# Loading two expert weights by column halves, and writing 1280 output rows by halves

## The chip, the cores and the metric

The kernel runs on one core of a Trainium2 chip. The metric is the device time of one execution in microseconds, given as the median of several runs. The core's engines work from queues of their own and wait for one another through semaphores: TensorE (PE, matrix products into PSUM), VectorE (DVE), ScalarE (ACT), GpSimd (Pool) and SyncE (SP). 16 DMA engines move data between HBM and on-chip memory. In this kernel Pool issues every load and SP issues every store.

## The reference

A block-selecting attention over 4 batches of 8 heads (768 positions, head size 64) is followed by a soft mixture of 8 experts with 4 slots each. `x` is the attention's output, 3072 rows of 512.

```python
logits = x @ phi                      # 3072 x 32
d = softmax(logits, axis=0)           # over all rows
slot_input = (d.T @ x).reshape(8, 4, 512)
for e in range(8):
    h = np.maximum(slot_input[e] @ w1[e], 0.0)    # 4 x 1024
    slot_out[e] = h @ w2[e]                       # 4 x 512
c = softmax(logits, axis=1)
out = c @ slot_out.reshape(32, 512)   # 3072 x 512, float32
```

Because `d` is normalised over all rows, no expert can start before the last head of the last batch is done, and no output row can be made before all of `h @ w2` is summed, except by column halves: a column of the output needs only the same column of every `w2`.

## The kernel before

The attention loop runs over 16 pairs of heads (`i` from 0 to 15); its parts for several pairs are interleaved in an order written out by hand, and each engine does its work in that order. The weights are loaded beside it. Of the 16 matrices (1 MB each in bf16, cast from 2 MB of float32 in HBM), indices 0 to 7 are `w1` and 8 to 15 are `w2` in the order `LATE`, so that index 15 is expert 4. Line numbers are those of the profile. `load_w` (L144) loads a whole matrix in one DMA. `wplan` says how many matrices are issued in which `i`; index 14 is issued in `i` = 14. Index 15 alone is loaded by column halves in `i` = 15 (`load_w_half`, L150): `w_last[1]` (columns 256 to 511) first, then `w_last[0]`, each in two DMAs of 256 KB. All loads are on Pool's queue, between masks and other small work of Pool, and land in order of issue.

After the loop comes the tail. The last batch's logits and their softmax are made, the slots' inputs go into `siT_pad`, and `experts_in` (L852) forms the hidden layer in two halves `f` of 512 columns. `relu` (L859, ACT) and `hidden_T` (L864 on PE, copies L868 on DVE) put it transposed into `hT_pad`. Pool clears `siT_pad` (L774), `hT_pad` (L778) and `zrow` (L821) ahead of that and adds two small copies to `zrow` (L838, L839), from which `slot_sums` (L872, L873) makes `zinv`, the slots' normalisation.

The second product has three parts. `experts_out` (L891) does experts 0 to 3 over all 512 columns, in groups of 16 matmuls for each `f`, into `so_ps`, one PSUM bank. `shared_out` (L911) does experts 5 to 7 and `last_expert_out` (L921) expert 4, both for one column half `y` at a time: half 1 adds to `so_ps[:, 256:]`, half 0 goes to a tile of its own, `so_last`. So half 1 is complete first (L955, ACT, scales it into `so_sb[1]`); half 0 needs ACT's `so_part` (L956), the shared part, the last weight's half 0, and one DVE operation (L974) that adds both.

The output has 12 blocks of 256 rows. Blocks 0 to 2 (`BYHALF = 3`) are made by column halves: `out_half` multiplies by one half of the slots' output (L967), DVE (L944) and ACT (L941) scale 128 rows each into `o_tiles[m]`, and SP stores 256 KB (L969). Half 1 of blocks 0 and 1 comes before half 0 is complete. Blocks 3 to 11 are made over all columns (L986) and stored in 512 KB (L992), the last one in two pieces (L990). The pool `op` has five buffers `o_sb`; a block can only be written into a buffer whose store has landed. After block 4, `last_rows` makes the weights of the last batch's rows: transposes (L534), a DVE copy (L542), column sums (L759) and their reciprocal (L879).

PSUM has 8 banks: two double tiles `sc`, two single tiles `tp`, one double tile `at`.

Of the kernel before, what the change touches and what calls it, by code (L numbers as in the profile page):

```python
# [9 lines left out]
F32 = mybir.dt.float32  # L10
BF16 = mybir.dt.bfloat16
ALU = mybir.AluOpType
# [5 lines left out]
CH = 32  # L18
NCHUNK = 24
NQT = 6  # L20
P = 128
# [38 lines left out]
def kernel(  # L60
# [82 lines left out]
            dst = w_sb[i].rearrange("p (a f) -> p a f", a=NFG // 4)  # L143
        nc.gpsimd.dma_start(out=dst, in_=src)  # L144

    def load_w_half(t, y):

        src = moe_w2[LATE[E - 1]].rearrange("(a p x) d -> a p x d", p=P, x=4)
        for a in range(NFG // 4):
            nc.gpsimd.dma_start(  # L150
                out=t[:, 4 * a:4 * a + 4, :], in_=src[a, :, :, y * Dm // 2:(y + 1) * Dm // 2])

    def load(i, nm, n=1):

# [396 lines left out]
            step(i // NPB)  # L551


    wplan = {2: 1, 3: 1, 4: 1, 5: 1, 6: 1, 8: 1, 9: 1, 10: 1, 11: 1, 12: 1, 13: 2, 14: 1, 15: 1}
    nw = 2

    def weights(i):
        nonlocal nw
        for _ in range(wplan.get(i, 0)):
            load_w(nw)  # L560
            nw += 1
# [56 lines left out]
    for i in range(1, NPAIR):  # L618
        slots = have(i - 3) and (i - 3) % NPB == NPB - 1
        if i >= EARLY:  # L620
            wt = ctx.enter_context(tc.tile_pool(name=f"wt{i}", bufs=1))
            if i < LAST:
                w_sb.append(wt.tile([P, NFG * Dm], BF16, name=f"w_sb{i}"))
                weights(i)
            else:
                w_last = [wt.tile([P, NFG, Dm // 2], BF16, name=f"w_last{y}") for y in range(2)]
                for y in (1, 0):
                    load_w_half(w_last[y], y)
        scores(i, 0)
        expo(i, 0)  # L630
        moe(moe_max, i - 3)
        scores(i, 1)
        expo(i, 1)
        if have(i + 1):
            ubound(i + 1)
        if i < LAST - 1:
            moe(moe_bound, i - 3)
        if have(i - 2):
            normalise(i - 2)
        if i == LAST - 1:  # L640
            moe(moe_bound, i - 3)
        if i == LAST:
            moe_ct_copy(B - 2)
        if have(i + 1):
            select(i + 1)
        moe(moe_comb, i - 3)
        if have(i + 2):
            transposes(i + 2, "k")
            evac_T(i + 2, "k")
        if not slots:  # L650
            if have(i + 2):
                load_v(i + 2)
            if i < EARLY:
                weights(i)
        if i != LAST - 1:
            pv(i - 1, [0, 1, 2])
        for g in (2, 3):
            scores(i, g)
            expo(i, g, not slots)
            if g == 2 and i == LAST - 1:  # L660
                pv(i - 1, [0, 1, 2])
            if g == 2 and i == LAST:
                x_transposes(i - 2)
        moe(moe_exp, i - 3)
        if slots:
            mask(i, 2)
            mask(i, 3)
        if have(i - 2) and i < LAST:
            x_transposes(i - 2)
        pv(i - 1, [3])  # L670
        if have(i + 2):
            transposes(i + 2, "q")
            evac_T(i + 2, "q")
            kmin(i + 2)
        if i < LAST - 1:
            moe(moe_exp2, i - 3)
        if have(i - 2):
            evac_x(i - 2)
        if have(i + 2):
            kmax(i + 2)  # L680
        if i < LAST - 1:
            moe(moe_scale, i - 3)
        if slots:
            if have(i + 2):
                load_v(i + 2)
            if i < EARLY:
                weights(i)
        scores(i, 4)
        expo(i, 4)
        if have(i + 5) and i % 2:  # L690
            load(i + 5, "k", 2)
            load(i + 5, "q", 2)
        if i == LAST - 1:
            moe(moe_exp2, i - 3)
            moe(moe_scale, i - 3)
        if i == LAST:
            pv(i - 1, [4, 5])
        moe(moe_comb2, i - 3)
        scores(i, 5)
        expo(i, 5)  # L700
        if have(i + 1):
            ns_transposes(i + 1)
            evac_ns(i + 1)
        if i < LAST:
            pv(i - 1, [4])
        moe(moe_dispatch, i - 3)
        if i < LAST:
            pv(i - 1, [5])
        if have(i + 2):
            qsplit(i + 2)  # L710
        if i < LAST - 1:
            moe(moe_ct, i - 4)
        elif i == LAST - 1:
            moe(moe_ct, i - 3)
        moe(moe_logits, i - 2)
        moe(moe_copy, i - 2)
        if i == LAST - 2:
            l_ctx.close()
        if i == LAST - 1:
            u_ctx.close()  # L720
# [50 lines left out]
    evac_x(LAST, 3, NQT)  # L771
    moe_logits(BL, range(NDG - 1), lg12)
    moe_logits(BL, range(NDG - 1, NDG), lg12)
    nc.gpsimd.memset(siT_pad, 0.0)  # L774
    i_ctx.close()
    tail = ctx.enter_context(tc.tile_pool(name="tail", bufs=1))
    hT_pad = tail.tile([P, NFG, E, CH], BF16, name="hT_pad")
    nc.gpsimd.memset(hT_pad, 0.0)  # L778
    m_old = m_run[(BL + 1) % 2]
    pm = small.tile([P, NS], F32, name="pm", tag="pm")  # L780
    nc.vector.tensor_reduce(pm, lg1.rearrange("p t s -> p s t"), axis=AX.X, op=ALU.max)
# [35 lines left out]
    keep(2)  # L817

    si = st.pop("si")
    zrow = tail.tile([1, 4, CH], F32, name="zrow")  # L820
    nc.gpsimd.memset(zrow, 1.0)  # L821
    for g in range(2):
        sl = slice(g * 16, (g + 1) * 16)
        nc.vector.tensor_tensor(
# [54 lines left out]
        nc.vector.reciprocal(inv_b, ps)  # L879

    HD = Dm // 2
    so_ps = p_at.tile([P, 2, 512], F32, name="so_ps", tag="at")[:, 0, :]
    so_last = p_sc.tile([P, HD], F32, name="so_last", tag="sc")
    so_part = tail.tile([P, HD], F32, name="so_part")

    hT = hT_pad.rearrange("p f e c -> p f (e c)")

    def experts_out(f):
        for fg in range(f * 4, (f + 1) * 4):
            for e in range(4):  # L890
                nc.tensor.matmul(  # L891
                    so_ps[e * CH:(e + 1) * CH, :], lhsT=hT_pad[:, fg, e, :],
                    rhs=w_sb[E + e][:, fg * Dm:(fg + 1) * Dm], start=(fg == 0), stop=(fg == NFG - 1),
                )

    outs = (so_last, so_ps[:, HD:])

    SHARED = [
        [(5, 0), (5, 1), (5, 2)],
# [5 lines left out]
    def shared_out(y, f):  # L905
        for n in range(3):
            for j in range(4):
                e, fg = SHARED[j][n]
                fg += f * 4
                c0 = e * CH - (SPE if j == e - 5 else 0)  # L910
                nc.tensor.matmul(  # L911
                    outs[y][j * CH:(j + 1) * CH, :], lhsT=hT[:, fg, c0:c0 + CH],
                    rhs=w_sb[E + LATE.index(e)][:, fg * Dm + y * HD:fg * Dm + (y + 1) * HD],
                    start=(y == 0 and f == 0 and n == 0), stop=False, skip_group_check=(y == 1),
                )

    def last_expert_out(y):
        c0 = 4 * CH - 2 * SPE
        for fg in range(NFG):
            j = fg % 4  # L920
            nc.tensor.matmul(  # L921
                outs[y][j * CH:(j + 1) * CH, :], lhsT=hT[:, fg, c0:c0 + CH],
                rhs=w_last[y][:, fg, :],
                start=False, stop=(fg >= NFG - 4), skip_group_check=(y == 1),
            )

    experts_in(0, 0)
# [17 lines left out]

    w_ctx.close()
    op = ctx.enter_context(tc.tile_pool(name="op", bufs=5))
    experts_out(0)
    hidden_T(1)
    shared_out(1, 0)  # L950
    slot_sums()
    experts_out(1)
    shared_out(1, 1)
    last_expert_out(1)
    nc.scalar.activation(so_sb[1], so_ps[:, HD:], func=ACT.Copy, scale=zinv)  # L955
    nc.scalar.activation(so_part, so_ps[:, :HD], func=ACT.Copy, scale=zinv)  # L956
    shared_out(0, 0)
    shared_out(0, 1)

    BYHALF = 3  # L960
    o_tiles = [op.tile([P, 2, Dm], F32, name="o_sb", tag="o_sb") for _ in range(BYHALF)]

    def out_half(m, y, tags):
# [4 lines left out]
            scaled(o_tiles[m][:, x, cols], ps, 2 * m + x)  # L968
        nc.sync.dma_start(out=rows(m)[:, :, cols], in_=o_tiles[m][:, :, cols])  # L969

    out_half(0, 1, ("tp", "tp"))
    out_half(1, 1, ("sc", "at"))
    last_expert_out(0)
    nc.vector.scalar_tensor_tensor(so_sb[0], so_last, zinv, so_part, op0=ALU.mult, op1=ALU.add)  # L974
    out_half(2, 1, ("tp", "tp"))
    out_half(0, 0, ("sc", "at"))
    out_half(1, 0, ("tp", "tp"))
    out_half(2, 0, ("sc", "at"))

    n = 0  # L980
    for m in range(BYHALF, NM):
        o_sb = op.tile([P, 2, Dm], F32, name="o_sb", tag="o_sb")
        for x, scaled in enumerate((scaled_act, scaled_dve)):
            tag = ("sc", "tp", "tp", "sc", "at")[n % 5]
            o_ps = homes[tag].tile([P, Dm], F32, name="o_ps", tag=tag)
            nc.tensor.matmul(o_ps, lhsT=cT[:, m, x], rhs=so_all, start=True, stop=True)  # L986
            scaled(o_sb[:, x, :], o_ps, 2 * m + x)
            n += 1
            if m == NM - 1:
                nc.sync.dma_start(out=rows(m)[:, x], in_=o_sb[:, x, :])  # L990
        if m < NM - 1:
            nc.sync.dma_start(out=rows(m), in_=o_sb)  # L992
        if m == 4:
            last_rows()


# [28 lines left out]
```

## Time and profile before

| | us |
|---|---|
| median of 3 runs | 159.59 (158.88 to 159.78) |
| profiled execution | 158.52 |
| its span | 156.8 |
| PE busy | 136.5 |
| ACT busy | 122.8 |
| DVE busy | 121.9 |
| Pool busy | 98.7 |

The span is the part of the execution in which the profile shows work; the profiled time has 1.7 us around it. The profile gives each engine's busy time, a strip of 40 slices of 3.92 us each, the chain of work that ended last, and groups of instructions by line. A row of the timeline reads: start, duration, engine, line, operation, output and input, count, and in brackets the idle time before it and what ended it. "SPq" and "POOL ... DMA_DIRECT2D" rows are the issuing of a transfer, not the transfer; a DMA row's last number is the time from issue to landing. A row of a table by stretches reads: stretch, its length, busy time and count of PE, PEld (weight loads), DVE, ACT and Pool, then TensorE's clock, the DMA engines' busy share and the GB/s that they moved.

### The profile page before, as it was taken

What the parts mean: (1) busy time and instruction counts of PE and PEld (TensorE: products, weight loads), DVE (VectorE), ACT (ScalarE), POOL (GpSimd) and SP (SyncE); (2) the same over time, 40 slices, a digit from 0 to 9 for tenths busy, and PEclk for the clock granted to TensorE, in tenths of its full rate; (3) what the DMA queues carried; (4) which work ended last, traced back from release to release, by engine and by line L of the source; (5) the groups of instructions that cost most, each with busy time, mean ns of one, the idle gap of its engine ahead of it and who ended that gap; (6) DMA issues with size and microseconds to landing.
All of it is one profiled execution on the core that took longest, in us unless ns stands there. A gap on an engine that the chain in (4) does not pass through costs nothing.

```text
span 156.8 us, 5988 instructions
## 1 busy us (share of the span) xinstructions
PE 136.5 (87%) x2464; PEld 93.2 (59%) x2464; DVE 121.9 (78%) x437; ACT 122.8 (78%) x171; POOL 98.7 (63%) x192
## 2 busy tenths in 40 slices
PE   7796789999999999999999899999979999977500
PEld 4463466767766776766777677766657854633100
DVE  5478887999999998999899899999753761178720
ACT  3479899999999889999989999998789532276520
POOL 6999647958877876697597975869696810000000
PEclk9999999999999999999999999999999999999975
DMA  2999999999999999999999999999999999949995
GB/s 37 160 172 195 194 193 221 172 201 203 196 214 199 201 202 207 204 197 210 186 198 205 205 203 201 208 200 198 211 197 216 212 215 198 151 158 399 419 420 223
DMA packets 43131, 32.92 MB, mean 210 GB/s; under 512 B 26208, under 2 KB 37984, under 8 KB 43104
## 3 DMA queue, kind: packets, MB, share of 16 engines
q0 software_dynamic: 40032, 26.25, 113.9%
q1 hardware_dynamic: 3072, 6.29, 10.3%
q8 instruction: 19, 0.31, 0.7%
q14 instruction: 8, 0.07, 0.1%
HBM read 52.49 MB, written 6.29 MB: 375 GB/s over the span
## 4 chain that ended last, share of the span: by engine, by line
PE 54%; ACT 18%; DVE 12%; issue 6%; DMA 5%; POOL 1%; DVEq 0%; ACTq 0%; POOLq 0%
ACT e_sb L349 11%; PE sc_ps L325 10%; PE at_ps L377 8%; PE sc_ps L335 7%; PE tr_ps L233 5%; PE xT_ps L399 4%; ACT qT L242 4%; DMA out_dram<-o_sb 3%; DMA q_in<-in_q_dram 3%; PE ub_ps L284 2%; PE h_ps L852 2%; PE ub_ps L277 2%; DVE x_sb L390 2%; DVE o_sb L944 1%; DVE mx L296 1%
## 5 line engine op out<-in xcount | busy, mean ns | idle before, releaser
L349 ACT ACTIVATE e_sb<-sc_ps 128x1024 bf16<-128x1024 f32 (+1 forms) x96 | 83.2, 919 | 6.0 <-PE sc_ps L335 5.5
L359 POOL TENSOR_SCALAR_AFFINE_SELECT e_sb<-e_sb 128x256 bf16<-128x256 bf16 x96 | 40.2, 437 | 17.6 <-ACT e_sb L349 17.4
L325 PE MATMUL sc_ps<-qT,kT 64*128 64x384 bf16 (+3 forms) x258 | 36.8, 306 | 2.9 <-ACT e_sb L349 2.2
L335 PE MATMUL sc_ps<-nsT,smask 64*128 64x384 bf16 (+2 forms) x294 | 38.1, 284 | 0.1
L377 PE MATMUL at_ps<-v_t,e_sb 128*128 128x65 bf16 x642 | 27.7, 193 | 0.9 <-PE sc_ps L335 0.6
L377 PEld LDWEIGHTS <-e_sb 128*128 128x128 bf16 x642 | 23.6, 97 | 3.5 <-issue 1.3
L325 PEld LDWEIGHTS <-kT 64*128 64x128 bf16 x258 | 14.0, 93 | 10.9 <-issue 5.5
L296 DVE MAX8 mx<-ub_ps 128x8 f32<-128x8 f32 (+1 forms) x192 | 16.8, 162 | 3.2 <-PE ub_ps L284 3.0
L164 POOL DMA_DIRECT2D v_t<-in_v_dram x16 | 16.7, 1044 | 3.6 <-PE xT_ps L399 1.8
L251 DVE TENSOR_REDUCE mm<-kT 128x24 bf16<-128x768 bf16 x16 | 15.1, 944 | 3.0 <-ACT kT L242 2.9
L335 PEld LDWEIGHTS <-smask 64*128 64x128 bf16 x294 | 15.0, 94 | 3.6 <-issue 0.6
L390 DVE TENSOR_TENSOR x_sb<-at_ps,inv 128x768 bf16<-128x768 f32 (+1 forms) x17 | 15.5, 910 | 0.6
L242 ACT COPY kT<-tr_ps 128x768 bf16<-128x768 bf16 x16 | 12.9, 804 | 3.5 <-PE tr_ps L233 3.5
L257 DVE TENSOR_REDUCE mm<-kT 128x24 bf16<-128x768 bf16 x16 | 15.1, 943 | 0.0
L242 ACT COPY qT<-tr_ps 128x768 bf16<-128x768 bf16 x16 | 12.8, 801 | 2.4 <-PE tr_ps L233 2.4
L144 POOL DMA_DIRECT2D w_sb<-in_moe_w_dram x15 | 10.7, 712 | 0.0
L410 DVE COPY xT_sb<-xT_ps 128x768 bf16<-128x768 bf16 (+1 forms) x15 | 8.0, 536 | 1.6 <-PE xT_ps L399 1.6
L233 PE MATMUL tr_ps<-ident,q_in 128*64 128x128 bf16 x192 | 8.4, 223 | 0.7 <-DMA q_in<-in_q_dram 0.5
L233 PE MATMUL tr_ps<-ident,k_in 128*64 128x128 bf16 x192 | 8.4, 223 | 0.5 <-DMA k_in<-in_k_dram 0.5
L399 PE MATMUL xT_ps<-ident,x_sb 128*128 128x128 bf16 x96 | 8.3, 221 | 0.4 <-DVE x_sb L390 0.3
L271 DVE TENSOR_SCALAR qpn<-qT 128x768 bf16<-128x768 bf16 x15 | 8.3, 553 | 0.0
L284 PE MATMUL ub_ps<-bd,qpn 128*128 128x48 bf16 x192 | 7.6, 183 | 0.4 <-DVE qpn L267 0.4
(147 smaller groups left out, 209.7 us busy)
## 6 DMA issues: line engine op xcount, KB each, us to landing
w_sb<-in_moe_w_dram POOLq DMA_DIRECT2D x15, 1024.0 KB, 16.3
out_dram<-o_sb SPq DMA_DIRECT2D x8, 512.0 KB, 4.6
v_t<-in_v_dram POOLq DMA_DIRECT2D x16, 192.0 KB, 12.4
k_in<-in_k_dram POOLq DMA_DIRECT2D x7, 384.0 KB, 11.8
q_in<-in_q_dram POOLq DMA_DIRECT2D x7, 384.0 KB, 13.0
out_dram<-o_sb SPq DMA_DIRECT2D x8, 256.0 KB, 2.9
w_last<-in_moe_w_dram POOLq DMA_DIRECT2D x4, 256.0 KB, 19.6
k_in<-in_k_dram POOLq DMA_DIRECT2D x2, 192.0 KB, 4.1
```

Of the source, the lines that this page charges most:

```text
L164: nc.gpsimd.dma_start(out=v_t[i % NV][:, :, :, :D], in_=v[b, 2 * j:2 * j + 2].rearrange("h (g p) d -> p h g d", p=P),)
L233: nc.tensor.matmul(ps[h * 64:(h + 1) * 64, g, :], lhsT=src[:, h, g * D:(g + 1) * D], rhs=ident, is_transpose=True,)
L242: nc.scalar.copy(t.rearrange("d (p g) -> d p g", g=NQT), st.pop((nm + "ps", i)).rearrange("d g p -> d p g"),)
L251: nc.vector.tensor_reduce(mm[:, 0, 0, :], kT, axis=AX.X, op=ALU.min)
L257: nc.vector.tensor_reduce(mm[:, 1, 0, :], kT, axis=AX.X, op=ALU.max)
L296: nc.vector.max(mx[:, a, :], ub[:, a, :max(8, 4 * t + 4)])
L325: nc.tensor.matmul(ps[:, h, c:c + w], lhsT=kT[r, kg * P:(kg + 1) * P], rhs=qT[r, qs], start=True, stop=False,)
L335: nc.tensor.matmul(ps[:, h, c + (f - t0) * P:c + (l - t0) * P], lhsT=smask[r, x, kg].rearrange("p a b -> p (a b)"), rhs=nsT[r, (f - x * NJ ...
L349: nc.scalar.activation(e[:, :, :w], st.pop(("scps", i, g))[:, :, :w], func=ACT.Exp, scale=scale)
L359: nc.gpsimd.affine_select(out=e[:, :, c:c + P], in_=e[:, :, c:c + P], compare_op=ALU.is_ge, fill=0.0, base=0, pattern=[[0, 2], [1, P]], ch ...
L377: nc.tensor.matmul(o, lhsT=st["e", i, g][:, h, c:c + P], rhs=v_t[i % NV][:, h, kg, :D + 1], start=(kg == 0), stop=(kg == t),)
L390: nc.vector.tensor_tensor(st["x", b][:, t0:t1, 2 * j:2 * j + 2, :].rearrange("p t h d -> p h t d"), at[:, :, :, :D], inv.broadcast_to([P, ...
```

## The change

The two last `w2` matrices (index 14, expert 7, and index 15, expert 4) are now both loaded by column halves. Half 1 of each is issued where the matrix was issued before (`i` = 14 and 15); half 0 of index 14 is issued after the last batch's logits, ahead of Pool's clearing of `siT_pad`, and half 0 of index 15 after the clearing of `zrow`, which moves up for that. Each half is two DMAs of 256 KB.

The whole second product is done by halves, each in a PSUM bank of its own (`so_ps[0]`, `so_ps[1]`), and half 1 ahead of most of half 0. `so_last`, `so_part` and the adding of the two are gone; half 0 is scaled by one DVE operation. Blocks 0 to 4 are made and stored by halves, which takes all five output buffers, and `last_rows` comes after block 5.

```diff
+    def load_w_half(i, y):
+        src = moe_w2[LATE[i - E]].rearrange("(a p x) d -> a p x d", p=P, x=4)
         for a in range(NFG // 4):
             nc.gpsimd.dma_start(
+                out=w_half[i][y][:, 4 * a:4 * a + 4, :], in_=src[a, :, :, y * Dm // 2:(y + 1) * Dm // 2])
...
-    wplan = {2: 1, 3: 1, 4: 1, 5: 1, 6: 1, 8: 1, 9: 1, 10: 1, 11: 1, 12: 1, 13: 2, 14: 1, 15: 1}
+    wplan = {2: 1, 3: 1, 4: 1, 5: 1, 6: 1, 8: 1, 9: 1, 10: 1, 11: 1, 12: 1, 13: 2}
...
         if i >= EARLY:
             wt = ctx.enter_context(tc.tile_pool(name=f"wt{i}", bufs=1))
-            if i < LAST:
-                w_sb.append(wt.tile([P, NFG * Dm], BF16, name=f"w_sb{i}"))
-                weights(i)
-            else:
-                w_last = [wt.tile([P, NFG, Dm // 2], BF16, name=f"w_last{y}") for y in range(2)]
-                for y in (1, 0):
-                    load_w_half(w_last[y], y)
+            w_half[i] = [wt.tile([P, NFG, Dm // 2], BF16, name=f"w_half{i}_{y}") for y in range(2)]
+            load_w_half(i, 1)
...
     moe_logits(BL, range(NDG - 1, NDG), lg12)
+    load_w_half(2 * E - 2, 0)
     nc.gpsimd.memset(siT_pad, 0.0)
...
     nc.gpsimd.memset(hT_pad, 0.0)
+    zrow = tail.tile([1, 4, CH], F32, name="zrow")
+    nc.gpsimd.memset(zrow, 1.0)
+    load_w_half(2 * E - 1, 0)
...
-    experts_out(0)
+    experts_out(1, range(4))
+    shared_out(1, 0)
     hidden_T(1)
-    shared_out(1, 0)
     slot_sums()
-    experts_out(1)
+    experts_out(0, range(2))
+    experts_out(1, range(4, NFG))
     shared_out(1, 1)
     last_expert_out(1)
-    nc.scalar.activation(so_sb[1], so_ps[:, HD:], func=ACT.Copy, scale=zinv)
-    nc.scalar.activation(so_part, so_ps[:, :HD], func=ACT.Copy, scale=zinv)
-    shared_out(0, 0)
-    shared_out(0, 1)
-
-    BYHALF = 3
+    nc.scalar.activation(so_sb[1], so_ps[1], func=ACT.Copy, scale=zinv)
+    experts_out(0, range(2, NFG))
+
+    BYHALF = 5
...
-    out_half(0, 1, ("tp", "tp"))
-    out_half(1, 1, ("sc", "at"))
+    pair_of = (("tp", "tp"), ("sc", "sc"))
+    for m in range(2):
+        out_half(m, 1, pair_of[m % 2])
+    shared_out(0, 0)
+    shared_out(0, 1)
+    for m in range(2, BYHALF):
+        out_half(m, 1, pair_of[m % 2])
     last_expert_out(0)
-    nc.vector.scalar_tensor_tensor(so_sb[0], so_last, zinv, so_part, op0=ALU.mult, op1=ALU.add)
-    out_half(2, 1, ("tp", "tp"))
-    out_half(0, 0, ("sc", "at"))
-    out_half(1, 0, ("tp", "tp"))
-    out_half(2, 0, ("sc", "at"))
+    nc.vector.tensor_scalar_mul(so_sb[0], so_ps[0], zinv)
+    for m in range(BYHALF):
+        out_half(m, 0, pair_of[(m + 1) % 2])
...
-        if m == 4:
+        if m == 5:
             last_rows()
```

In `experts_out(y, fgs)`, `shared_out(y, f)` and `last_expert_out(y)` the output is `so_ps[y]` throughout, and a helper `w2(i, fg, y)` picks the 256 columns of a weight from its half tile or from the whole matrix.

More of the change, by code (lines that the diff above doesn't have):

```diff
@@ L144, in load_w @@
         nc.gpsimd.dma_start(out=dst, in_=src)
-    def load_w_half(t, y):
-        src = moe_w2[LATE[E - 1]].rearrange("(a p x) d -> a p x d", p=P, x=4)
+    def load_w_half(i, y):
+        src = moe_w2[LATE[i - E]].rearrange("(a p x) d -> a p x d", p=P, x=4)
         for a in range(NFG // 4):
             nc.gpsimd.dma_start(
-                out=t[:, 4 * a:4 * a + 4, :], in_=src[a, :, :, y * Dm // 2:(y + 1) * Dm // 2])
+                out=w_half[i][y][:, 4 * a:4 * a + 4, :], in_=src[a, :, :, y * Dm // 2:(y + 1) * Dm // 2])
     def load(i, nm, n=1):
@@ L551, in moe @@
             step(i // NPB)
-    wplan = {2: 1, 3: 1, 4: 1, 5: 1, 6: 1, 8: 1, 9: 1, 10: 1, 11: 1, 12: 1, 13: 2, 14: 1, 15: 1}
+    wplan = {2: 1, 3: 1, 4: 1, 5: 1, 6: 1, 8: 1, 9: 1, 10: 1, 11: 1, 12: 1, 13: 2}
     nw = 2
+    w_half = {}
     def weights(i):
@@ L819 @@
     si = st.pop("si")
-    zrow = tail.tile([1, 4, CH], F32, name="zrow")
-    nc.gpsimd.memset(zrow, 1.0)
     for g in range(2):
@@ L881, with w2, experts_out @@
     HD = Dm // 2
-    so_ps = p_at.tile([P, 2, 512], F32, name="so_ps", tag="at")[:, 0, :]
-    so_last = p_sc.tile([P, HD], F32, name="so_last", tag="sc")
-    so_part = tail.tile([P, HD], F32, name="so_part")
+    so_t = p_at.tile([P, 2, 512], F32, name="so_ps", tag="at")
+    so_ps = [so_t[:, y, :HD] for y in range(2)]
     hT = hT_pad.rearrange("p f e c -> p f (e c)")
-    def experts_out(f):
-        for fg in range(f * 4, (f + 1) * 4):
+    def w2(i, fg, y):
+        if i in w_half:
+            return w_half[i][y][:, fg, :]
+        return w_sb[i][:, fg * Dm + y * HD:fg * Dm + (y + 1) * HD]
+    def experts_out(y, fgs):
+        for fg in fgs:
             for e in range(4):
                 nc.tensor.matmul(
-                    so_ps[e * CH:(e + 1) * CH, :], lhsT=hT_pad[:, fg, e, :],
-                    rhs=w_sb[E + e][:, fg * Dm:(fg + 1) * Dm], start=(fg == 0), stop=(fg == NFG - 1),
+                    so_ps[y][e * CH:(e + 1) * CH, :], lhsT=hT_pad[:, fg, e, :], rhs=w2(E + e, fg, y),
+                    start=(fg == 0), stop=False,
                 )
-    outs = (so_last, so_ps[:, HD:])
     SHARED = [
@@ L911, in shared_out @@
                 nc.tensor.matmul(
-                    outs[y][j * CH:(j + 1) * CH, :], lhsT=hT[:, fg, c0:c0 + CH],
-                    rhs=w_sb[E + LATE.index(e)][:, fg * Dm + y * HD:fg * Dm + (y + 1) * HD],
-                    start=(y == 0 and f == 0 and n == 0), stop=False, skip_group_check=(y == 1),
+                    so_ps[y][j * CH:(j + 1) * CH, :], lhsT=hT[:, fg, c0:c0 + CH],
+                    rhs=w2(E + LATE.index(e), fg, y), start=False, stop=False,
                 )
@@ L921, in last_expert_out @@
             nc.tensor.matmul(
-                outs[y][j * CH:(j + 1) * CH, :], lhsT=hT[:, fg, c0:c0 + CH],
-                rhs=w_last[y][:, fg, :],
-                start=False, stop=(fg >= NFG - 4), skip_group_check=(y == 1),
+                so_ps[y][j * CH:(j + 1) * CH, :], lhsT=hT[:, fg, c0:c0 + CH],
+                rhs=w2(2 * E - 1, fg, y), start=False, stop=(fg >= NFG - 4),
             )
```

## The prediction

> **What bounds the kernel now.** I read the 40-slice strip first, then the chain of waits from 134 us on, then engines and DMA by stretches of the tail, last the rows of single transfers. The strip:
>
> ```profile
> DMA  2999999999999999999999999999999999949995
> GB/s 37 160 172 195 194 193 221 172 201 203 196 214 199 201 202 207 204 197 210 186 198 205 205 203 201 208 200 198 211 197 216 212 215 198 151 158 399 419 420 223
> ```
>
> The 16 DMA engines are full throughout: inputs at about 205 GB/s up to slice 33, the output at 420 GB/s from slice 36. Only slices 34 and 35 sag, where loads hand over to stores. The change works there. The tail in stretches (the last two columns are DMA share and GB/s):
>
> ```profile
> 135.00:138.20 3.20, 2.84 (x68) 1.81 (x61) 0.97 (x3) 1.61 (x4) 0.00 (x0) 1.00 0.70 96
> 138.20:139.20 1.00, 0.62 (x6) 0.31 (x6) 0.37 (x1) 0.18 (x2) 0.00 (x0) 1.00 0.00 0
> 139.20:140.60 1.40, 1.06 (x7) 0.68 (x7) 1.40 (x5) 1.17 (x3) 0.00 (x0) 1.00 1.02 359
> 140.60:141.00 0.40, 0.40 (x3) 0.20 (x2) 0.35 (x1) 0.40 (x3) 0.00 (x0) 1.00 0.27 87
> 141.00:143.60 2.60, 1.53 (x17) 0.78 (x15) 2.09 (x4) 1.25 (x3) 0.00 (x0) 1.00 1.07 375
> 143.60:154.80 11.20, 3.70 (x13) 1.07 (x11) 5.07 (x7) 4.59 (x7) 0.00 (x0) 0.83 1.03 419
> ```
>
> Loads thin out from 135 and are gone at 138.2; nothing moves for 1.0 us; two half stores flow; a hole of 0.4; from 141.0 the engines are full to the end, near 155.0. From 141 on the kernel is bound by store bytes: a half store (256 KB, 262,144 bytes) is 0.70 us of traffic at 375 GB/s, a full one (512 KB) 1.25 us at 419. So the question is when stores start and whether the queue ever runs dry. The chain of waits (start, duration, what):
>
> ```profile
> 132.93 0.86 PE so_ps L891 x16
> 134.89 0.98 PE so_ps L891 x16
> 135.86 0.33 PE so_ps L911 x12
> 136.19 0.22 PE so_ps L921 x8
> 136.41 0.66 PE so_last L911 x24
> 137.06 0.34 PE oh_ps L967 x2
> 138.83 0.49 DVE so_all L974
> ```
>
> **Earlier first store.** A 512-wide group of 16 takes 0.86 to 0.98 us, so a 256-wide one 0.43 to 0.49 (24 such take 0.66, 12 take 0.33, 8 take 0.22). New order from 132.93: 16 half matmuls (0.43) and 12 shared (0.33) to 133.69.
>
> ```profile
> 132.98 0.60 ACT L859 ACTIVATE h_sb<-h_ps 128x512 bf16<-128x512 f32 x1 [1.53 <-PE h_ps L852]
> 133.72 0.26 PEld L864 LDWEIGHTS <-h_sb 128*128 128x128 bf16 x4 [0.42 <-ACT h_sb L859]
> 134.51 0.38 PE L872 MATMUL z_ps<-identf,zrow 1*128 1x1 f32 x2
> 137.98 0.63 SPq L969 DMA_DIRECT2D out_dram<-o_sb  x1
> ```
>
> The ReLU of the second hidden half ends at 133.58, so its transposes start at 133.72 and end near 134.07. The slot sums (0.31 of the 0.38 are on the chain) run to 134.38; 8 matmuls of the first half fill the wait for DVE's copy to 134.60; then 16 (0.49), 12 (0.33) and 8 (0.22): the second half is summed at 135.64 instead of 136.41. ACT scales it behind the remaining 24 (0.66), and the first output product starts at 136.30 instead of 137.06. The first store moves by 0.76, from 137.98 to 137.22. Issue to first traffic is 1.2 us (137.98 against the stretch that starts at 139.20), so stores flow from 138.42.
>
> **Later last load.** On Pool's queue the weights land in order of issue:
>
> ```profile
> 105.97 1.41 POOL L144 DMA_DIRECT2D w_sb<-in_moe_w_dram  x2
> w_sb<-in_moe_w_dram POOLq DMA_DIRECT2D x1, 1024.0 KB, 17.0
> w_sb<-in_moe_w_dram POOLq DMA_DIRECT2D x2, 1024.0 KB, 19.2
> 109.10 0.72 POOL L144 DMA_DIRECT2D w_sb<-in_moe_w_dram  x1
> w_sb<-in_moe_w_dram POOLq DMA_DIRECT2D x1, 1024.0 KB, 23.9
> L150 POOL DMA_DIRECT2D w_last<-in_moe_w_dram x4: 742/742/823, 115.6 to 117.9; - x4
> DMA to landing us min/median/max: 18.9/19.6/20.5
> ```
>
> Of the two issued from 105.97 one needs 17.0 and the pair's median is 19.2, so the other needs 21.4 and lands at 128.1. The weight issued at 109.10 lands at 133.0, 4.9 us later. The four half pieces end at 117.9 + 20.5 = 138.4, 5.4 us later for the same megabyte. A second weight in halves therefore puts the last landing 0.5 later, at 138.9 (bounds 0 and 0.5). Each quarter takes about 1.35 us: column half 1 of both weights is there at 133.5, 1.9 us before it is used; half 0 of the first one at 136.2, before the shared products that now stand between outputs 1 and 2 (about 136.8). Whether stores that flow from 138.42 hold up the last pieces, no row shows, as the two kinds hardly overlap: 0 at best, 1.0 if the last 0.5 us of loads shares each engine with larger store packets; I take 0.2, nearer the lower end since few pieces are left by then. Last landing 139.1.
>
> **Pool.** The two issues added at 109 and the two that leave 115.6 fall beside its idle time or only make masks earlier. Later it works in order:
>
> ```profile
> 122.66 0.41 POOL L359 TENSOR_SCALAR_AFFINE_SELECT e_sb<-e_sb 128x256 bf16<-128x256 bf16 x1 [0.65 <-ACT e_sb L349]
> 123.01 0.95 POOL L774 MEMSET siT_pad<- 128x1024 bf16 x1
> 123.90 1.80 POOL L778 MEMSET hT_pad<- 128x2048 bf16 x1
> 128.56 0.35 DVE L824 TENSOR_TENSOR siT_pad<-si_acc,si_ps 128x64 bf16<-128x64 f32 x2 [0.31 <-PE si_ps L515]
> 129.65 0.18 POOL L838 COPY zrow<-zrow 1x12 f32<-1x12 f32 x1 [3.81 <-DVE zrow L833]
> ```
>
> Two issues of 0.74 put the first memset at 124.5 and the last at 127.5; DVE wants them from 128.56 on, and without that cover up to 1.5 us would show. [...] From 127.5 to 138.9 are 11 us of loads at 0.2 MB/us; all but the last 0.5 MB of that is queued by then, so the queue doesn't run dry. Cost nothing; the removed scaling of so_part was off the path too.
>
> **From the last landing to the end.** This is where the change loses.
>
> ```profile
> 138.43 0.29 PE L921 MATMUL so_last<-w_last,hT_pad 128*32 128x256 bf16 x4 [0.58 <-DMA w_last<-in_moe_w_dram]
> 138.83 0.48 DVE L974 SCALAR_TENSOR_TENSOR so_all<-so_last,zinv,so_part 128x256 bf16<-128x256 f32 x1 [0.64 <-ACT o_sb L941]
> 139.79 0.47 ACT L941 ACTIVATE o_sb<-oh_ps,inv_a 128x256 f32<-128x256 f32 x1 [0.23 <-PE oh_ps L967]
> L944 DVE TENSOR_SCALAR o_sb<-oh_ps,inv_a 128x256 f32<-128x256 f32 x6 | 2.6, 477 | 2.2 <-PE oh_ps L967 2.2
> out_dram<-o_sb SPq DMA_DIRECT2D x4, 256.0 KB, 2.9
> 142.43 0.56 DVE L542 COPY cT_all<-cT_ps 128x768 bf16<-128x768 bf16 x1
> 143.04 0.30 PE L759 MATMUL cs_ps<-live,cT_all 128*128 128x1 bf16 x6 [0.65 <-DVE cT_all L542]
> 143.90 0.75 DVE L944 TENSOR_SCALAR o_sb<-o_ps,inv_a 128x512 f32<-128x512 f32 x1 [0.32 <-PE o_ps L986]
> 144.71 0.33 SPq L992 DMA_DIRECT2D out_dram<-o_sb  x1
> ```
>
> Landing to DVE start is 0.4 (138.43 to 138.83): 139.5. DVE is free, its five half outputs of 0.477 end near 139.25. Scaling 0.48; from its end (139.31 before) to the end of the first evacuation (140.26) 0.95; issue 0.05: first half-0 store at 141.0. Half-1 stores flow from 138.42 for 5 x 0.70 to 141.9; the next start at 142.2: a hole of 0.3.
>
> All five output buffers are now taken by halves. Output 5 needs buffer 0, which is free when the first half-0 store has landed: 141.0 + 2.9 = 143.9. Behind the waiting evacuations stand, on DVE, the copy of the last batch's weights (the m == 5 work) and everything after it; PE's column sums wait for that copy, and output 6 is behind them. Before, this work ran while two full stores were queued, their buffers free. Output 5: evacuation 0.75, issue at 144.7, flow at 145.9; the half-0 stores end at 142.2 + 3.5 = 145.7. Output 6: DVE's copy from 144.65 (0.56), 0.05 to the sums (0.30), 0.56 until DVE starts (143.34 to 143.90), 0.75, 0.06: issue at 146.95, flow at 148.15. Output 5 has drained at 147.15, so the DMA engines stand for 1.0 us. After that six stores, 7.5 us, in a full queue: end at 155.65.
>
> Before, the end is near 155.0: 139.2 + 6 x 0.70 + 0.4 + 9 x 1.25 = 155.05. Change +0.6 to +0.65. The profiled run, span 156.8 and 158.52 with what lies around it, would become 159.17; it stands 1.07 below the median 159.59, which becomes 160.24, said as 160.2. Bounds about that: sharing and landing of the loads -0.25 (DVE is busy till 139.25 anyway) to +0.8; landing of a 256 KB store -0.4 to +0.2 (from 2.5, were nothing queued ahead, to 3.1); lag of a full store, which has fewer pieces, -0.2 to 0. Together -0.85 to +1.0: own range 159.4 to 161.3.
>
> [...]
>
> **Rivals.** *The holes close.* If the first half-0 store lands sooner and the sums at m == 5 hide, stores run from 138.42 without a gap: 7.0 + 8.75 us end at 154.2, 0.85 earlier: 158.7. [...] *Stores hold up the last loads.* If each late load piece waits for a store packet, the full 1.0 instead of 0.2 goes through the same line: +1.45, 161.0. It decides once loads are still moving at 138.4. [...] *The first half isn't earlier.* If narrow matmuls were paced by weight loads, the second half would be ready at 136.4 as before; the five DVE outputs then end at 140.0, and the line runs 0.5 later than mine: +1.15, 160.7. Against it: 24 narrow ones in 0.66.
>
> **How the numbers follow.** Forecast 0.62, holes close 0.16, loads held up 0.12, no earlier half 0.06, rest 0.04. A run can tell 0.5% (0.8 us) from no change. Over +0.8: 0.29 of the forecast's 0.62 (its middle is just under), all of the second and third rival, 0.02 of the rest: 0.49. Below -0.8: 0.10 of the closing holes (their middle is just beyond), 0.02 of the rest: 0.12. Within: 0.39. The range 158.6 to 161.4 reaches over the closed holes and the held-up loads and leaves out about 0.2: the outer parts of these two and most of the rest.
>
> **What would show it.** First store issued near 137.2, last weight landed near 139, the first full store near 144.7, the next over 2 us behind it with DMA standing between, then 420 GB/s to the end. Wrong if outputs 5 and 6 are issued under 1.3 us apart, if half-1 weights are waited for, or if PE's half sums don't end near 135.6.

## The result, and the profile after

| | before | changed |
|---|---|---|
| median of 13 runs, us | 159.32 | 160.64 |
| lowest to highest | 158.63 to 159.89 | 160.30 to 162.66 |
| profiled execution (its span) | 158.52 (156.8) | 161.08 (159.4) |

The ratio of the changed kernel to the one before is 1.010, with a 95% interval of 1.0069 to 1.013: slower by about 1.3 us between the medians. The forecast was +0.65 us, inside a range that holds the result; the direction was right and the size about half of it. The two profiled executions are 2.56 us apart. The one before lies 0.8 below its median and the one after 0.4 above, and the changed kernel's tail begins 0.42 us later in its trace (DVE's last `inv` L389 at 123.95 instead of 123.53). The 0.42 us are there before anything that the change touches: Pool issues the two weights of 105.97 at 106.39. Where the two traces are compared below, that 0.42 is taken off.

The strip of 40 slices of the changed kernel (each 3.98 us):

```profile
PEclk9999999999999999999999999999999999998675
DMA  2999999999999999999999999999999999589695
GB/s 34 167 169 201 189 199 219 174 194 210 196 210 199 206 197 212 199 202 195 194 207 195 212 197 203 202 206 204 201 207 214 202 195 195 75 306 351 282 420 222
```

Before, two slices sagged where loads hand over to stores (151 and 158 GB/s), and then 399 and more. Now the handover goes down to 75, and there is a second sag, 282, three slices behind it, at 147.4 to 151.4 us. The 75 looks worse than it is, because the slices fall otherwise: over the same six microseconds, 135 to 141 us on the clock of before, the engines carried 128 GB/s now and 141 before. TensorE's clock drops in the same place. The stretches of the changed kernel there (columns as before; the last three are clock, DMA share, GB/s):

```profile
145.00:146.00 1.00, 0.00 (x0) 0.00 (x0) 0.19 (x1) 0.21 (x1) 0.00 (x0) 1.00 1.09 383
146.00:147.00 1.00, 0.00 (x0) 0.00 (x0) 1.00 (x2) 0.48 (x1) 0.00 (x0) 0.79 1.09 386
147.00:148.00 1.00, 0.91 (x8) 0.44 (x9) 0.22 (x2) 0.06 (x1) 0.00 (x0) 0.50 0.66 263
148.00:149.00 1.00, 1.00 (x4) 0.37 (x3) 0.62 (x1) 0.83 (x2) 0.00 (x0) 0.50 0.74 303
149.00:150.00 1.00, 1.00 (x4) 0.38 (x3) 0.88 (x2) 0.83 (x2) 0.00 (x0) 0.51 0.01 4
```

The DMA engines, which carried 418 to 422 GB/s in each of the last four of these microseconds before, are a quarter to a third idle in two of them and stand in the last. The timeline of the changed kernel shows why, from the evacuation of block 5 to the store of block 6:

```profile
145.81 0.75 DVE L942 TENSOR_SCALAR o_sb<-o_ps,inv_a 128x512 f32<-128x512 f32 x1 [2.23 <-DMA out_dram<-o_sb]
146.48 0.55 DVE L542 COPY cT_all<-cT_ps 128x768 bf16<-128x768 bf16 x1
146.63 0.34 SPq L992 DMA_DIRECT2D out_dram<-o_sb  x1
147.09 0.32 PE L755 MATMUL cs_ps<-live,cT_all 128*128 128x1 bf16 x6 [2.43 <-DVE cT_all L542]
147.94 0.69 ACT L939 ACTIVATE o_sb<-o_ps,inv_a 128x512 f32<-128x512 f32 x1 [1.46 <-PE o_ps L986]
148.38 0.75 DVE L942 TENSOR_SCALAR o_sb<-o_ps,inv_a 128x512 f32<-128x512 f32 x1 [0.74 <-DMA out_dram<-o_sb]
149.19 0.34 SPq L992 DMA_DIRECT2D out_dram<-o_sb  x1
```

DVE stands for 2.23 us until a store has landed that holds block 5's buffer, and PE stands for 2.43 us behind it, because the copy L542 stands behind that evacuation on DVE. Block 5's store is issued at 146.63, block 6's at 149.19: 2.56 us apart, while one full store is 1.25 us of traffic. The bracket on DVE's last row must be read with care. It names a store, but ACT writes into the same buffer from 147.94 on, so the buffer was free by then; DVE waited for its product from PE.

The early end of half 1 is there, but nothing comes of it. The chain of waits in the changed kernel:

```profile
135.87 0.25 PE so_ps L920 x8
136.12 0.02 issue
136.14 0.48 ACT so_all L954
136.62 0.04 issue
136.66 0.84 PE so_ps L893 x24
137.50 0.55 PE oh_ps L964 x4
```

Half 1 is summed at 136.12 (135.70 on the clock of before; predicted 135.64). Then PE doesn't go on with the 24 matmuls of half 0: they start when ACT has scaled half 1. The timeline names it in brackets, and gives the first store:

```profile
136.66 0.84 PE L893 MATMUL so_ps<-w_sb,hT_pad 128*32 128x256 bf16 x24 [0.58 <-ACT so_all L954]
138.41 0.63 SPq L966 DMA_DIRECT2D out_dram<-o_sb  x1
139.16 1.06 SPq L966 DMA_DIRECT2D out_dram<-o_sb  x1
142.34 0.59 SPq L966 DMA_DIRECT2D out_dram<-o_sb  x1
```

So the first store is issued at 138.41, on the clock of before 137.99: as before (137.98). The third row above is the first half-0 store.

### The profile page after: what moved, and what is told of

Read it like the earlier page. It is cut to its first block, busy times and chain, and to the rows that moved or that the text cites. A ratio compares the mean times of both kernels' runs of the same rounds, so it can differ in the third digit from the quotient of the medians.

```text
span 159.4 us, 6074 instructions
## 1 busy us (share of the span) xinstructions
PE 138.4 (87%) x2500; PEld 94.9 (60%) x2500; DVE 122.2 (77%) x439; ACT 123.1 (77%) x172; POOL 100.5 (63%) x195
## 4 chain that ended last, share of the span: by engine, by line
PE 49%; ACT 17%; DMA 14%; DVE 6%; issue 6%; POOL 2%; DVEq 1%; ACTq 0%; POOLq 0%
DMA k_in<-in_k_dram 12%; ACT e_sb L349 11%; PE sc_ps L325 8%; PE at_ps L377 7%; PE sc_ps L335 6%; PE tr_ps L233 5%; PE xT_ps L399 4%; ACT qT L242 4%; PE h_ps L850 2%; PE ub_ps L284 2%; DMA out_dram<-o_sb 2%; PE o_ps L986 2%; DVE o_sb L942 2%; PE ub_ps L277 1%; PE warm_ps L224 1%
## 5 line engine op out<-in xcount | busy, mean ns | idle before, releaser
L144 POOL DMA_DIRECT2D w_sb<-in_moe_w_dram x14 | 9.9, 711 | 0.0
```

## The experiments

All times are medians, with the ratio to the kernel before, run on the same chip beside it. The changed kernel's 1.010 (1.0069 to 1.013) is what most of them are held against.

**Where the last rows' work stands.** Nothing but the place of `last_rows` changes: ahead of block 5.

```diff
     for m in range(BYHALF):
         out_half(m, 0, pair_of[(m + 1) % 2])
+    last_rows()
...
-        if m == 5:
-            last_rows()
```

> The changed kernel, but the last batch's row weights (transposes, DVE copy, column sums, reciprocal) are made right after the half-0 outputs of block 4 instead of behind block 5. Theory A (outputs 5 and 6 stand in one line: buffer, copy, column sums): this work falls into the time in which block 5 waits for its buffer, block 6 is issued under 1.3 us behind block 5 instead of 2.6, the stretch without traffic ahead of 150 us closes, and the time falls by 1.0 to 1.4 us, to about 159.4. Theory B (the loss is the late start of the stores alone): block 6 comes earlier but the time falls by under 0.4 us.

Measured: 159.46 us, ratio 1.0012 (0.999 to 1.0034). The loss is gone, as far as the medians can tell. SP's rows of blocks 5 and 6 in this run, and the stretches:

```profile
146.47 0.34 SPq L993 DMA_DIRECT2D out_dram<-o_sb  x1
147.33 0.34 SPq L993 DMA_DIRECT2D out_dram<-o_sb  x1
```

```profile
147.00:148.00 1.00, 1.00 (x4) 0.39 (x3) 0.96 (x2) 0.83 (x2) 0.00 (x0) 0.50 0.75 306
148.00:149.00 1.00, 1.00 (x5) 0.39 (x4) 0.90 (x3) 0.83 (x2) 0.00 (x0) 0.68 1.01 414
149.00:150.00 1.00, 0.75 (x4) 0.12 (x2) 1.00 (x2) 0.97 (x2) 0.00 (x0) 1.00 1.06 434
```

Blocks 5 and 6 go out 0.86 us apart. The small hole ahead of block 5 (306 GB/s) stays, the large one behind it is closed.

The other direction: the same work two blocks later (`if m == 7`).

> The changed kernel with the last rows' work behind block 7 instead of 5, nothing else. Theory A says that the same line of copy, sums and output is free where full stores are queued: blocks 5 to 7 are issued 0.7 to 0.9 us apart and each is 1.25 us of traffic, so over 1 us is queued when the line begins, and the stretch near 149 us without traffic goes; 1.0 to 1.4 us below the changed kernel, within 0.4 of before. Rival (the work costs its time wherever it stands): the gap moves behind block 7, less than 0.5 us gained.

Measured: 159.66 us, ratio 1.003 (1.0005 to 1.0054). SP's rows of blocks 7 and 8, and the DMA engines meanwhile:

```profile
148.63 0.33 SPq L992 DMA_DIRECT2D out_dram<-o_sb  x1
150.96 0.33 SPq L992 DMA_DIRECT2D out_dram<-o_sb  x1
```

```profile
149.00:150.00 1.00, 0.86 (x9) 0.46 (x10) 0.23 (x2) 0.29 (x1) 0.00 (x0) 1.00 1.00 410
150.00:151.00 1.00, 0.96 (x6) 0.34 (x4) 0.85 (x2) 1.00 (x3) 0.00 (x0) 1.00 1.04 426
```

The issues are still 2.33 us apart, but the DMA engines carry 410 and 426 GB/s all the while: three full stores are queued when the line begins (issued at 147.28, 147.94 and 148.63). The same work costs 1.4 us behind block 5 and some 0.5 us two blocks on. This trace is of the longest of the twelve executions (160.82 us); its stores start late, at 139.74, for a reason that stays open, so only the stretch behind block 7 is read from it.

**Five halves put into the kernel before**, with its own loads and second product.

```diff
-    BYHALF = 3
+    BYHALF = 5
...
     out_half(2, 1, ("tp", "tp"))
-    out_half(0, 0, ("sc", "at"))
-    out_half(1, 0, ("tp", "tp"))
-    out_half(2, 0, ("sc", "at"))
+    out_half(3, 1, ("sc", "at"))
+    out_half(4, 1, ("tp", "tp"))
+    for m in range(BYHALF):
+        out_half(m, 0, (("sc", "at"), ("tp", "tp"))[m % 2])
...
-        if m == 4:
+        if m == 5:
```

> The kernel before with blocks 0 to 4 by halves and the last rows' work behind block 5; loads and second product as before. Theory A: the hole between blocks 5 and 6 appears here too, 1.0 to 1.6 us slower than before, about 160.6. Rival (the loads in halves or the split second product cost the time): within 0.3 us of before.

Measured: 160.8 us, ratio 1.0094 (1.006 to 1.0128), as much as the whole change. SP's rows of blocks 5 and 6 and the emptiest stretch behind block 5 are those of the changed kernel over again:

```profile
146.53 0.53 SPq L993 DMA_DIRECT2D out_dram<-o_sb  x1
149.09 0.34 SPq L993 DMA_DIRECT2D out_dram<-o_sb  x1
```

```profile
149.00:150.00 1.00, 1.00 (x4) 0.30 (x2) 0.85 (x3) 0.79 (x2) 0.00 (x0) 0.50 0.11 41
```

Not all of the 0.94% need be that hole. In this trace the engines also thin out before the half-0 stores, to 98 and 223 GB/s in the two microseconds from 141, where the changed kernel's carry 382 and 373.

**Three halves in the changed kernel** (`BYHALF = 3`, `if m == 4`), loads and second product as changed.

> The changed kernel with blocks 0 to 2 by halves and the last rows' work behind block 4, as before; loads and second product as changed. Theory A: two full blocks go out from free buffers ahead of the line of copy and sums, so no stretch without traffic: within 0.5 us of the kernel before, 0.8 to 1.6 below the changed one. Rival (loads or second product cost part of the loss): 0.5 us or more above before.

Measured: 159.45 us, ratio 1.0026 (1.0001 to 1.0051): the loss but for a quarter of a per cent is gone from this side too.

**The loads alone**, put into the kernel before: index 14 by halves, both halves 0 issued late, `zrow` moved up.

```diff
+            w_half[i] = [wt.tile([P, NFG, Dm // 2], BF16, name=f"w_half{i}_{y}") for y in range(2)]
+            load_w_half(i, 1)
...
+    load_w_half(2 * E - 2, 0)
     nc.gpsimd.memset(siT_pad, 0.0)
...
+    load_w_half(2 * E - 1, 0)
```

> The kernel before with only the loads changed: index 14 in column halves too, half 0 of both weights issued late; products, outputs and the place of the last rows' work as before. My forecast's term for the loads (last landing 0.5 us later): last weight lands near 139 and the half-0 line starts up to 0.5 us later, which the full store queue hides for the most part: 0 to 0.4 us slower. Rival (the earlier half 1 or the relief of Pool helps): faster by 0.2 us or more.

Measured: 159.43 us, ratio 1.0007 (0.9983 to 1.003). In its trace DVE scales half 0 from 139.78, against 138.83 before; 0.31 of that is a later tail, 0.64 the later weight. The medians can't be told apart, as expected. That the queue of stores hides the later weight isn't shown, for the engines all but stand once in this trace:

```profile
141.00:142.00 1.00, 0.83 (x5) 0.39 (x4) 0.90 (x3) 1.00 (x4) 0.00 (x0) 1.00 0.09 24
```

**A tile for each half sum.** `so_ps[0]` moves to the pool `sc`, `so_ps[1]` stays in `at`.

```diff
-    so_t = p_at.tile([P, 2, 512], F32, name="so_ps", tag="at")
-    so_ps = [so_t[:, y, :HD] for y in range(2)]
+    so_ps = [p_sc.tile([P, HD], F32, name="so_ps0", tag="sc"), p_at.tile([P, HD], F32, name="so_ps1", tag="at")]
...
-    pair_of = (("tp", "tp"), ("sc", "sc"))
+    pair_of = (("tp", "tp"), ("sc", "at"))
```

> The changed kernel with the two halves of the second product in two PSUM tiles of their own pools instead of two banks of one tile, so that the 24 matmuls of half 0 need not wait until ACT has scaled half 1 (PE stood 0.54 us there). Theory A plus this wait: the first store is issued 0.7 us earlier against the sum of half 1, the half-0 chain starts 0.5 us earlier, and as everything behind it is one line, the time falls by 0.4 to 0.7 us. Rival (stores and loads, not PE, set the half-0 chain): no change beyond 0.2 us.

Measured: 160.17 us, ratio 1.0028 (1.0005 to 1.0051), below the changed kernel's interval. From its timeline the 24 matmuls, the first store and DVE's scaling of half 0, and its emptiest stretch behind block 5:

```profile
135.77 0.83 PE L892 MATMUL so_ps<-w_sb,hT_pad 128*32 128x256 bf16 x24
137.50 0.63 SPq L965 DMA_DIRECT2D out_dram<-o_sb  x1
139.64 0.48 DVE L975 TENSOR_SCALAR so_all<-so_ps,zinv 128x256 bf16<-128x256 f32 x1
```

```profile
148.00:149.00 1.00, 1.00 (x4) 0.43 (x3) 0.96 (x2) 0.78 (x2) 0.00 (x0) 0.50 0.02 8
```

No wait stands in brackets, and the first store leaves at 137.50, 0.91 earlier than in the changed kernel. Its tail starts 0.27 later than before, so that is 137.23 on the clock of before, and half 0 is scaled from 139.37. The hole behind block 5 is as deep as ever; it has only moved forward with the line.

**Eight output buffers instead of five.**

> The changed kernel with 8 output buffers instead of 5. Theory A: blocks 5, 6 and 7 wait for no landing, block 5 is issued near 144.5 in place of 146.6, the work at m == 5 runs while half stores are queued, no hole; 1.2 to 1.7 us less than the changed kernel, about 159.2. Theory B: under 0.4 us less.

Measured: 160.26 us (159.23 to 161.43), ratio 1.0041 (1.0011 to 1.007), a likely gain (the intervals just touch), but less than expected and not the hole's end. SP's last half store and blocks 5 and 6, and the emptiest stretch behind block 5:

```profile
145.38 0.57 SPq L966 DMA_DIRECT2D out_dram<-o_sb  x1
146.61 0.35 SPq L992 DMA_DIRECT2D out_dram<-o_sb  x1
149.11 0.34 SPq L992 DMA_DIRECT2D out_dram<-o_sb  x1
```

```profile
149.00:150.00 1.00, 1.00 (x4) 0.36 (x3) 0.80 (x2) 0.79 (x2) 0.00 (x0) 0.50 0.07 29
```

Block 5 waits for no landing now, and still it is issued at 146.61, not at 144.5: its products stand behind the half-0 outputs on PE, whose clock in this execution is 0.50 from about 143.4 on. And block 6 is 2.50 us behind it with all the buffers it wants: in this execution the line of copy, sums and output makes the large hole without a buffer's wait.

This execution doesn't stand for all twelve, however. By TensorE's mean granted clock they fall into two groups: seven at 0.957 to 0.964 took 160.22 to 161.43 us (the traced one, 161.00, is among them), and five at 0.974 to 0.982 took 159.23 to 159.92, with a median of 159.53 where the kernel before had 159.49. The three executions of the changed kernel at 0.979 and 0.980 took 160.31 to 160.87. So where the clock stays up, eight buffers seem to take most of the loss away. No such execution was traced, and that the clock is the cause of the two groups isn't shown.

**TensorE's clock.** Ten matmuls that nobody reads are put on PE between the transposes and the column sums, where it stands for 2.4 us.

```diff
         moe_ct(BL)
+        dummy = p_at.tile([P, 512], F32, name="dummy", tag="at")
+        for _ in range(10):
+            nc.tensor.matmul(dummy, lhsT=ident, rhs=so_all, start=True, stop=True)
```

> The changed kernel with 10 matmuls of 128x512 whose result nobody reads, on PE between the transposes and the column sums behind block 5, where PE stands for 2.4 us. Theory C (part of the hole is TensorE's clock, 0.50 from 146.8 us on, which stretches the products of block 6): the clock stays at 1.00 through blocks 5 to 7, DVE starts block 6 about 0.6 us behind the sums instead of 1.0, and the time falls by 0.3 to 0.5 us. Theory A alone: same time within 0.2 us, as the line copy, sums, output stays.

Measured: 160.37 us, ratio 1.0068 (1.0041 to 1.0095). The sums in the chain of waits, then DVE's start and SP's issues in the timeline, then the emptiest stretch behind block 5:

```profile
146.82 0.22 PE cs_ps L755 x6
```

```profile
147.59 1.41 DVE L945 TENSOR_SCALAR o_sb<-o_ps,inv_a 128x512 f32<-128x512 f32 x2 [0.32 <-PE o_ps L989]
146.28 0.34 SPq L995 DMA_DIRECT2D out_dram<-o_sb  x1
148.41 0.34 SPq L995 DMA_DIRECT2D out_dram<-o_sb  x1
```

```profile
148.00:149.00 1.00, 1.00 (x4) 0.29 (x3) 1.00 (x3) 1.00 (x3) 0.00 (x0) 1.00 0.40 160
```

The clock stays at 1.00, DVE starts block 6 at 0.55 us behind the sums' end (147.04) instead of 0.97, and the issues are 2.13 apart instead of 2.56. The hole is there but shallower. The trace shows the 0.4 us; the two intervals overlap, so the gain in time is likely and not shown. Nor is the clock the main part of the loss: with it at 1.00 the kernel is still 0.68% slower than before.

**Looking for a version below both.** Both mends together: a tile for each half sum, and the last rows' work ahead of block 5.

> The changed kernel with both mends: half sums in tiles of their own and the last rows' work ahead of block 5. If the two effects (each seen alone: 1.4 and 0.7 us below the changed kernel on average) lie in one line they add: about 158.7, 0.7 us below before. Rival (the stores are bytes-bound once the hole is gone, and start only 0.75 us earlier): 0.3 to 0.7 below before. Neither expects it above before.

Measured: 159.28 us, ratio 0.9983 (0.9958 to 1.0009). The effects don't add in full. In its trace the five early stores are issued from 137.52 to 140.54, and the next only at 142.27, because the last weight, issued at 129.74, lands 10.48 us later, at 140.22. The rows of its chain:

```profile
129.74 10.48 DMA w_half<-in_moe_w_dram
140.27 0.32 PE so_ps L919 x4
140.61 0.49 DVE so_all L975
```

That weight is issued 1.04 us later than in the kernel with a tile for each half alone (128.70), which accounts for its later landing. This is also the longest of the twelve executions (160.14; the shortest took 158.46), and it has a second hole, ahead of block 5:

```profile
147.00:148.00 1.00, 1.00 (x5) 0.37 (x4) 1.00 (x2) 1.00 (x3) 0.00 (x0) 1.00 0.17 70
```

The same with four blocks by halves, and one with three:

> Half sums in tiles of their own, blocks 0 to 3 by halves, the last rows' work ahead of block 4. Looking for a version below both: first store near 137.6, a free buffer for block 4, two fewer half stores than the version with five: 0.2 to 0.8 us below before. If the last weight's landing sets the half-0 line, not the first store, it equals before within 0.3.

> Half sums in tiles of their own, blocks 0 to 2 by halves, the last rows' work behind block 4. 0.75 us earlier first store than before, but the early half stores are used up (3 x 0.70) before half 0 is there, so a hole opens ahead of it: 0 to 0.5 us below before.

Measured: four, 160.72 us, ratio 1.0075 (1.0032 to 1.0118), a miss; three, 159.43 us, ratio 1.0005 (0.9973 to 1.0037). With four the last weight lands at 140.1 too, and the queue runs dry twice, ahead of half 0 and ahead of block 4. Two rows of it:

```profile
142.00:143.00 1.00, 0.59 (x3) 0.23 (x3) 0.96 (x3) 1.00 (x3) 0.00 (x0) 1.00 0.07 24
146.00:147.00 1.00, 1.00 (x4) 0.43 (x3) 0.84 (x2) 0.74 (x2) 0.00 (x0) 0.50 0.00 0
```

Here too the executions differ with the mean clock: five at 0.958 to 0.961 took 160.37 to 161.10 us (the traced one is the longest), two at 0.979 and 0.981 took 159.86 and 159.58. Part of the miss may be that.

No version tried is below the kernel before by more than the measurement can tell.

## Why the prediction was right in direction and short in size

*The line behind block 5: right, and moving it takes the loss away.* The prediction put the slowing into one line (landing, evacuation, copy, sums, output of block 6) behind which the DMA engines stand. Moving that work ahead of block 5 takes the loss away (1.0012), moving it two blocks on does nearly as much (1.003), and putting five halves into the kernel before brings as much (1.0094, though with another thin stretch in its trace). How much of it is the buffer's wait stays open: with eight buffers blocks 5 and 6 are still 2.50 us apart in the traced execution, but the five executions at a higher clock took about as long as the kernel before.

*Earlier first store, 0.76: failed.* "ACT scales it behind the remaining 24" took the matmuls of half 0 and ACT's reading of half 1 to run side by side. They write and read two banks of one tile, and in the built program the matmuls wait for ACT (0.58 us in the timeline). The half sum itself was right to 0.06 us (135.70 against 135.64). So the first store didn't move, and the half-0 line, which I had start from the last weight's landing, started from PE and DVE instead: DVE scaled half 0 from 140.45, on the clock of before 140.03, not 139.5. With a tile for each half the first store came at 137.23 on that clock, where the sum had it at 137.22, DVE scaled half 0 from 139.37 (sum: 139.5), and the kernel was 0.28% slower than before (0.05 to 0.51%), which the forecast of 0.4% fits.

*Later last load: right, and of no weight in this kernel.* The last quarter was issued at 128.78 and landed 10.6 us later, near 139.4, on the clock of before 139.0 (predicted 138.9 to 139.1); PE used it only at 139.92, without a wait. The sum has no cost for Pool; in the trace its last issue, at 128.78, stood for 0.33 us until an earlier `w_sb` weight had landed, and the first copy to `zrow` behind it waited for DVE (0.55), so nothing shows a cost. The loads alone cost nothing that the medians can tell (1.0007). The sum's 0.2 us for stores that hold up the last pieces, and the 1.0 of its rival, were my choice, and no run shows them. The rival of held-up loads could hardly come here: the stores' traffic starts 1.2 us behind the first issue, near 139.6, when the last weight has landed. With a tile for each half the stores start 0.91 us earlier, and the last weight, issued at 128.70, lands 10.6 us later, near 139.3, no later than here. In the two versions where it landed at 140.1 and 140.2 it was also issued about 1 us later (129.6 and 129.74) and took no longer (10.5).

*Landing of a half store, 2.9: too short.* The first half-0 store, issued at 142.34, held block 5's buffer until 145.69, 3.35 us, beyond the bound of 3.1. The chain of waits has it as:

```profile
142.34 3.35 DMA out_dram<-o_sb
```

The ten half stores of the changed kernel took 2.9 to 3.4 us from issue to landing, 3.3 in the median; the six of the kernel before 2.5 to 2.9.

*From block 5 to block 6, 2.25: too short by 0.31.* Here the clock comes in, which the prediction didn't have. At full clock, with the extra matmuls, it is 2.13, 0.12 less than predicted.

*The sum.* On the clock of before, block 6 was issued at 148.77 where the sum had 146.95, 1.8 us late. The first half-0 store gives 0.92 of that (141.92 for 141.0): 0.53 from DVE's later start, the rest from SP, which had the late half-1 stores still to issue, 0.68 apart, after its second issue had taken 1.06. The landing gives 0.45, the clock 0.31, and 0.14 is spread over the rest. These are the sizes of one execution that lies above its median; between the medians the forecast of +0.65 falls short by 0.67. So the mis-sized term is the start of the half-0 line first, and it failed at the step of the earlier first store.

*The other rivals.* "The holes close" is refuted by the stretch at 4 GB/s. "The first half isn't earlier" came true in its result, the first store, but not by its mechanism: the narrow matmuls do run at half to two thirds of the wide ones' cost (24 in 0.66 to 0.84 and 16 in 0.44, where 16 wide ones took 0.86 to 0.98).

## What to carry to other kernels

Work that only has to be done some time, such as `last_rows`, goes where a queue behind it is full. In this kernel it cost nothing that the medians can tell in front of the first block that waits for a buffer, 0.5 us or less behind two or three queued stores, and 1.4 us between the two. Splitting an accumulator over two banks freed nothing here while both banks belonged to one tile and so to one wait (0.58 us, gone with a tile for each half): look at what the built program waits for, engine by engine, before giving the overlap a value. A trace is of one execution: hold its time and clock against the others before a cause is read from it. And an earlier first store is worth only what the next thing in line, here the last weight, allows.

## What the hardware showed that was not expected

TensorE's granted clock fell to 0.50 in the changed kernel from about 146.6 to 150.0 us (0.79 in the microsecond from 146, 0.51 in that from 149). The drop began while PE stood for 2.43 us, 1.9 us behind the end of its last matmul (144.66); PE was busy again from 147.09, and the clock stayed at 0.50 for 2.9 us more. From the end of its column sums it took 0.97 us until DVE could start on the products of block 6, 0.55 with the clock held at 1.00. The kernel before never falls below 1.00 until its matrix work is over: its last matmul ends at 148.38, and the clock is at 1.00 until 151.0. What sets the moment of the drop isn't shown. The executions with eight buffers spread from 159.23 to 161.43 us, the longer ones at the lower mean clock, and no run here shows the cause of that either.

A store's issue on SP took 1.06 us (the second, at 139.16 in the changed kernel), where its neighbours took 0.56 to 0.63, and that delayed the third store. With a tile for each half the second took 1.14, with the last rows' work ahead of block 5 it took 0.53. It isn't tied to loads in flight: with five halves in the kernel before, the fourth took 1.05 from 141.29, behind the last weight's use. Its cause stays open.
